# Two dense layers after an attention: a shorter activation chain, next tokens split part by part, and an even rate of weight conversion

## The chip, the cores and the metric

The kernel runs on one core of one Trainium2 chip. The metric is the time of one execution on the device in microseconds (us). The engines of the core work side by side, each through its own list of instructions in order: TensorE (PE, the matrix products), VectorE (DVE), ScalarE (ACT), GpSimd (POOL), and SyncE (SP), which here issues the transfers (DMA). Matrix products go into PSUM banks, from which VectorE and ScalarE read; all else lies in SBUF. An engine that reaches an instruction whose data or buffer is not ready waits there, and all that stands behind it in its list waits too.

## The reference, cut to what matters

```python
scores = q @ k.T / 8                       # 4 batches x 8 heads, 576 tokens, 64 wide
thresh = max(scores) - tau                 # per row
attn   = softmax(where(scores >= thresh, scores, -1e9))
x      = (attn @ v) as 2304 tokens x 512
h = x @ w_in                               # first layer, 512 -> 2048
g = where(h >= 1, h, where(h <= -1, 0, (h + 1)**2 / 4))
x = g @ w_out                              # 2048 -> 512
h = x @ w_in2                              # second layer, same sizes
out = (h * clip(h + 3, 0, 6) / 6) @ w_out2
```

## The kernel before, in words

**Numbers in two parts.** Every operand of a matrix product in the dense layers is kept as a high and a low half (`xh`/`xl` for tokens, `wih`/`wil` and `woh`/`wol` for weights, `gh`/`gl` for activations), and a product is three matrix products: high with high, high with low, low with high. So tokens and weights are *split* before use. Splitting one token part (128 rows by up to 512 tokens; a group of tokens has four parts, one for each value of `kk`) is a transfer into `xst` (three buffers), a copy on ScalarE (L521) and a subtraction on VectorE (L522).

**Weights.** Each of the 64 weight pieces (two layers, 16 slices `f`, one piece of `w_in` and one of `w_out` for each slice) is converted from 64-bit numbers. A piece takes two *halves* of work: the first (`split_a`) is two ScalarE operations (L115, L124), three VectorE ones (L125, L128, L130) and one on GpSimd (L132); the second (`split_b`) is one on ScalarE (L138) and one on GpSimd (L140). The raw pieces have three buffers, and the load of a piece is put into SyncE's list up to three pieces ahead. While the attention runs, L119 and L121 stand in place of L124 and L125.

**Order of work.** First comes the attention. From the end of its first batch on, the first layer's work for slices 0 to 9 of the first batches (groups of 256 tokens, 60 steps, `dense1`) is threaded through it. Then `dense` runs the rest of the first layer (`seq2`): 16 steps for token group 3 (512 tokens wide), 16 for group 4 (256 wide), and 6 each for groups 0, 1 and 2 (512 wide, slices 10 to 15 alone). Then it runs the second layer: 80 steps, groups in the order 3, 0, 1, 4, 2. A step takes one group and one slice: `em_h` makes twelve matrix products into one of four PSUM banks Q, then the activation (first layer: L548 VectorE, L549 ScalarE, L550 VectorE; second layer: L552 ScalarE, L553 VectorE), then the split of the result (`gh` L556 on ScalarE, `gl` L557 on GpSimd). The products with `w_out` (L581) follow two steps later (MLAG = 2) and add up in PSUM banks P; after the last slice of a group the sums are copied out (`ob`: L622, L624, L626 in the first layer, L632 and L634 in the second), and only then can the next group's products start in those banks.

**What sets the order.** The program emits a step's work in the order of the code: `ahead2` or `ahead3` (weight halves), `em_h`, the split of the next group's tokens, the products of two steps ago. A scheduler then puts each engine's list in order, by times that it models, so an engine's list is not the order of the code. In the first layer `ahead2` gives up to two halves a step, as long as the number of pieces stays under a limit: the limit rises by two pieces a step from step 20 on (in group 4, as the buffers of slices 0 to 9 come free for the second layer's weights), stops after ten steps' worth, and rises again in the last steps. In the second layer `ahead3` gives four halves a step until all are converted.

Of the kernel before, what the change touches and what calls it, by code (L numbers as in the profile page):

```python
# [10 lines left out]
ACTF = mybir.ActivationFunctionType  # L11
ALU = mybir.AluOpType
# [6 lines left out]
def kernel(  # L19
# [13 lines left out]
    V, S, G, T = nc.vector, nc.scalar, nc.gpsimd, nc.tensor  # L33
    NB, NH, SEQ, D = q.shape
    NT, DM = out.shape
    HP = NH // 2
    KD = DM // 128
    KF = DM * 4 // 128
# [9 lines left out]
    NF1 = 10  # L48
    MLAG = 2
# [16 lines left out]
    half = const.tile([128, 1], F32, name="half")  # L66
# [5 lines left out]
    def narrow(t, g):  # L72
        return t[g // 2][:, :, (g % 2) * GRP:(g % 2 + 1) * GRP]

    def f32(ap):
        return ap.bitcast(F32)

    def bank(tag):
        return ps.tile([128, 512], F32, tag=tag, name=tag)
# [104 lines left out]
    weights = Weights()  # L184
# [317 lines left out]
    xs, gs, acc, cnt = {}, {}, {}, {"h": 0, "a": 0}  # L502
    wide = {}
    H_TAGS = ["Q2"]

    def split_x(key):
        m, g, ph = key
        r = []
        for kk in range(KD):
            if ph == 1:  # L510
                if kk % 2 == 0:
                    t = mt.tile([128, 2, GRP], F32, tag="io", name="xst", bufs=2)
                    nc.sync.dma_start(out=t, in_=narrow(xd, g)[:, kk:kk + 2, :])
                pool, n, bufs, src = mt, GRP, 1, t[:, kk % 2]
            else:
                pool, n, bufs = wide["x"], WIDE[g], 2
                src = pool.tile([128, n], F32, tag="xst", name="xst", bufs=3)
                nc.sync.dma_start(out=src, in_=(x2d if m == 1 else xd)[g][:, kk, :])
            hi = pool.tile([128, n], F32R, tag=f"xh{kk}", name="xh", bufs=bufs)
            lo = pool.tile([128, n], F32R, tag=f"xl{kk}", name="xl", bufs=bufs)  # L520
            S.activation(out=hi, in_=src, func=ACTF.Copy)  # L521
            V.tensor_tensor(out=lo, in0=src, in1=f32(hi), op=ALU.subtract)  # L522
            r.append((hi, lo))
        xs[key] = r

    def pin_mlp(mm):
        if mode["att"]:
            after(mm, pe_pins[-2])

    def em_h(key, m, f):  # L530
        cnt["h"] += 1
        n = GRP if key[2] == 1 else WIDE[key[1]]
        h = bank(H_TAGS[cnt["h"] % len(H_TAGS)])[:, 0:n]
        wh, wl = wsp["i", m, f]
        x = 0
        for kk in range(KD):
            xh, xl = xs[key][kk]
            for l, r in ((wh, xh), (wh, xl), (wl, xh)):
                mm = T.matmul(h, l[:, kk * 128:(kk + 1) * 128], r, start=(x == 0), stop=(x == 3 * KD - 1))  # L539
                if x % 3 == 0:  # L540
                    pin_mlp(mm)
                x += 1
            if kk < KD - 1:
                yield 0.33
        hp_, hb = (mt, HOLD) if key[2] == 1 else (wide["g"], MLAG + 1)
        r = hp_.tile([128, n], F32, tag="r", name="r", bufs=2)
        if m == 0:
            V.tensor_scalar(out=r, in0=h, scalar1=1.0, scalar2=-1.0, op0=ALU.min, op1=ALU.max)  # L548
            S.activation(out=r, in_=r, func=ACTF.Square, scale=0.5, bias=half)  # L549
            vlast = V.tensor_tensor(out=r, in0=h, in1=r, op=ALU.max)  # L550
        else:
            S.activation(out=r, in_=h, func=ACTF.Relu, bias=three)  # L552
            vlast = V.scalar_tensor_tensor(out=r, in0=r, scalar=6.0, in1=h, op0=ALU.min, op1=ALU.mult)  # L553
        gh = hp_.tile([128, n], F32R, tag="gh", name="gh", bufs=hb)
        gl = hp_.tile([128, n], F32R, tag="gl", name="gl", bufs=hb)
        x = S.activation(out=gh, in_=r, func=ACTF.Copy)  # L556
        y = G.tensor_tensor(out=gl, in0=r, in1=f32(gh), op=ALU.subtract)  # L557
        gs[key, f] = (gh, gl)
        if not mode["att"]:
            pins.update(S=x, V=vlast, G=y)  # L560

    def blocks(m, g):

        return KD if m == 0 else WIDE[g] // 128

    def em_out(key, m, f, first, last, fin, i):

        gh, gl = gs[key, f]
        wh, wl = wsp["o", m, f]
        if first:  # L570
            if i % 2 == 0:
                acc[key, i // 2] = pair_bank(f"P{i // 2}")
        c = slice(i * 128, (i + 1) * 128)
        if m == 0:
            a = acc[key, i // 2][:, i % 2, 0:WIDE[key[1]]]
            ops = (wh[:, c], gh), (wh[:, c], gl), (wl[:, c], gh)
        else:
            a = acc[key, i // 2][:, i % 2]
            ops = (gh[:, c], wh), (gh[:, c], wl), (gl[:, c], wh)
        for x, (l, r) in enumerate(ops):  # L580
            T.matmul(a, l, r, start=(first and x == 0), stop=(last and x == 2))  # L581
        if last:
            fin(key[1], a, i)
# [30 lines left out]
    def load_part(g):  # L614
        for i in range(KD):
            pbs[g, i] = wide["p"].tile([128, WIDE[g]], F32, tag="pb", name="pb", bufs=KD)
            nc.sync.dma_start(out=pbs[g, i], in_=x2p[g][:, i, :])
# [31 lines left out]
    while o < len(outs):  # L649
        n = len(steps)  # L650
# [30 lines left out]
    def behind():  # L681

        for l in steps[n_h:]:
            for g, half, f in l:
                for _ in em_part((0, g, 1), half, f):
                    pass
                yield

    def dense(m, ph, seq, fin, ahead, following, rest=None):

        fs = {}
        for g, f in seq:
            fs.setdefault(g, []).append(f)
        splits = [(m, g, ph) for g in fs] + following

        def out_block(n, i):
            g, f = seq[n]
            em_out((m, g, ph), m, f, f == fs[g][0], f == fs[g][-1], fin, i)
            if i == blocks(m, g) - 1:
                del gs[(m, g, ph), f]  # L700

        for n, (g, f) in enumerate(seq):
            key = (m, g, ph)
            if key not in xs:
                split_x(key)
            ahead(n, g, f)
            for c in em_h(key, m, f):
                pass
            if rest is not None:
                rest(n)  # L710
            if m == 0 and g < NB - 1 and f == fs[g][-3]:
                load_part(g)
            if f == fs[g][-2]:
                for nxt in splits[splits.index(key) + 1:][:1]:
                    split_x(nxt)
            if f == fs[g][-1]:
                xs.pop(key)
            if n >= MLAG:
                for i in range(blocks(m, seq[n - MLAG][0])):
                    out_block(n - MLAG, i)  # L720
        for i in range(blocks(m, seq[-1][0])):
            for n in range(len(seq) - MLAG, len(seq)):
                out_block(n, i)
# [29 lines left out]
    fs2 = list(range(NF1, KF))  # L753
# [33 lines left out]
    NLATE = 2  # L787
# [12 lines left out]
    seq2 = [(g, f) for g in (NB - 1, NB) for f in range(KF)]  # L800
    n_free = len(seq2) - KF + MLAG + 1
    seq2 += [(g, f) for g in range(NB - 1) for f in fs2]
    n_last = len(seq2) - len(fs2) + MLAG + 1
    left = behind()
    SWITCH = MLAG + 2

    def rest(n):

        if n <= MLAG:
            for _ in range(100 if n == MLAG else 4):  # L810
                if next(left, 0) == 0:
                    break
        if n == MLAG:
            H_TAGS[:] = ["Q0", "Q1", "Q2", "Q3"]
            mt_es.close()
            wide["p"] = ctx.enter_context(tc.tile_pool(name="mt2", bufs=1, side="right"))
            wide["g2"] = ctx.enter_context(tc.tile_pool(name="g2", bufs=1, side="right"))

    def ahead2(n, g, f):
        if n == SWITCH:  # L820
            wide["g"] = wide["g2"]
        if n == SWITCH + MLAG + 1:
            g_es.close()
            late = ctx.enter_context(tc.tile_pool(name="wlate", bufs=1))
            for x in range(KF - NLATE, KF):
                wpool[x] = late
        limit = 2 * KF if n > SWITCH + MLAG else 2 * (KF - NLATE)
        limit += 2 * max(0, min(n - n_free, NF1)) + 2 * max(0, n - n_last)
        for _ in range(2):
            if weights.done < limit:  # L830
                weights.half()
        if g == NB - 1:
            weights.upto(2 * f + 2)

    def ahead3(n, g, f):
        for _ in range(4):
            weights.half()
        weights.upto(2 * KF + 2 * n + 2)

    order3 = [NB - 1, *range(NB - 2), NB, NB - 2]  # L840
# [31 lines left out]
```

## Time and profile before

| what | value |
|---|---|
| time, median of 3 runs | 1221.02 us (1218.41 to 1221.44) |
| the profiled execution: its own time | 1220.3 us |
| its span in the trace | 1218.5 us |
| TensorE busy / weight loads | 95% / 81% of the span |
| VectorE, ScalarE, GpSimd busy | 59%, 55%, 59% |
| mean granted clock of TensorE | 0.990 |

The span runs from the first to the last instruction in the trace; 1.8 us of the execution's time lie around it. Busy shares are means over stages with different limits, so they say little by themselves: the attention, up to about 515 us, has all four engines between 78% and 91% busy, and the stretch after 846 us has TensorE alone busy. TensorE's granted clock is given as a share of full speed (2.4 GHz); its only other level is half of that.

### The profile page before, as it was taken

The page shows a single profiled execution, that of the slowest core. Times are in us where ns is not written, and L with a number is a line of the kernel's source. Part 1 is how long each engine was busy: PE and PEld are TensorE (multiplying, and loading weights), DVE is VectorE, ACT ScalarE, POOL GpSimd, SP SyncE. Part 2 cuts the span into 40 slices and gives each one's busy share as a digit, 9 for nine tenths or more (in the row PEclk, how much of TensorE's full clock was granted, in tenths as well). Part 3 has the DMA queues.
Part 4 walks back from the last instruction along what each step waited for, and adds up shares of the span by engine and source line. Part 5 has one row for each costly group of instructions (what it writes and reads, how often), then busy time and mean ns, then how long its engine had stood idle before and what let it go on. Part 6 is the DMA issues. An engine that isn't in the chain of part 4 may idle for free. (4 is left out here: it accounts for less than half of the span.)

```text
span 1218.5 us, 19295 instructions
## 1 busy us (share of the span) xinstructions
PE 1160.1 (95%) x6820; PEld 992.8 (81%) x6820; DVE 715.1 (59%) x1543; ACT 667.1 (55%) x1222; POOL 724.7 (59%) x745
## 2 busy tenths in 40 slices
PE   7899999999999899989999988998999999999998
PEld 5666678998898899989889976886888888888886
DVE  6999989988888889484344797466321121121111
ACT  6777778788788688564334665345332232232222
POOL 5887699999899899665342877347522222222221
PEclk9999999999999999989999999999999999999999
DMA  6444431121121220142112454444010010010000
GB/s 161 129 129 120 135 111 51 48 77 50 49 76 46 64 72 31 53 146 74 61 53 70 120 165 133 135 135 142 1 31 26 1 43 23 1 44 1 18 1 35
DMA packets 99857, 87.08 MB, mean 71 GB/s; under 512 B 51376, under 2 KB 83632, under 8 KB 99760
## 3 DMA queue, kind: packets, MB, share of 16 engines
q1 hardware_dynamic: 99760, 85.85, 23.9%
q8 instruction: 54, 0.88, 0.3%
q14 instruction: 43, 0.35, 0.1%
HBM read 68.52 MB, written 17.30 MB: 70 GB/s over the span
## 5 line engine op out<-in xcount | busy, mean ns | idle before, releaser
L557 POOL TENSOR_TENSOR gl<-r,gh 128x512 fp32r<-128x512 f32 (+1 forms) x190 | 205.0, 1080 | 380.9 <-ACT gh L556 365.8
L539 PE MATMUL Q<-xh,wih 128*128 128x512 f32 (+1 forms) x760 | 262.3, 345 | 0.9 <-ACT xh L521 0.7
L539 PE MATMUL Q<-xl,wih 128*128 128x512 f32 (+1 forms) x760 | 259.5, 341 | 1.4 <-DVE xl L522 1.4
L539 PE MATMUL Q<-xh,wil 128*128 128x512 f32 (+1 forms) x760 | 258.8, 341 | 0.0
L553 DVE SCALAR_TENSOR_TENSOR r<-r,Q 128x512 f32<-128x512 f32 (+1 forms) x80 | 50.8, 634 | 270.4 <-ACT r L552 270.2
L539 PEld LDWEIGHTS Q<-xh,wih 128*128 128x128 f32 x760 | 145.7, 192 | 19.3 <-ACT xh L521 1.4
L539 PEld LDWEIGHTS Q<-xl,wih 128*128 128x128 f32 x760 | 145.7, 192 | 18.4 <-DVE xl L522 1.9
L334 DVE SCALAR_TENSOR_TENSOR p<-p,th,e 128x576 f32<-128x576 f32 x144 | 152.0, 1057 | 11.1 <-ACT e L330 8.9
L539 PEld LDWEIGHTS Q<-xh,wil 128*128 128x128 f32 x760 | 145.7, 192 | 15.7
L556 ACT ACTIVATE gh<-r 128x512 fp32r<-128x512 f32 (+1 forms) x190 | 99.3, 523 | 101.9 <-PE P L581 40.1
L380 POOL TENSOR_TENSOR Gl<-pf,Gh 128x512 fp32r<-128x512 f32 (+1 forms) x110 | 146.2, 1329 | 10.0 <-ACT Gh L379 3.3
L552 ACT ACTIVATE r<-Q,three 128x512 f32<-128x512 f32 (+1 forms) x80 | 51.5, 644 | 162.0 <-PE Q L539 157.8
L330 ACT ACTIVATE e<-p,nm 128x576 f32<-128x576 f32 x144 | 110.9, 772 | 34.6 <-DVE p L329 33.4
L581 PE MATMUL P<-woh,gh 128*128 128x512 f32 x288 | 112.9, 394 | 5.1 <-DVE ob L622 3.9
L329 DVE TENSOR_SCALAR_CACHE_REDUCE p<-P 128x576 f32<-128x576 f32 x144 | 107.5, 748 | 12.6 <-PE P L305 6.9
L318 PE MATMUL P<-kst,qh 128*128 128x288 f32 x320 | 99.3, 326 | 14.6 <-DVE xu L451 5.4
L581 PE MATMUL P<-wol,gh 128*128 128x512 f32 x288 | 112.8, 392 | 0.0
L581 PE MATMUL P<-woh,gl 128*128 128x512 f32 x288 | 111.3, 391 | 0.0
L132 POOL TENSOR_TENSOR w_c<-w_c,w_raw 128x512 int32<-128x512 int32 x64 | 87.8, 1371 | 35.2 <-issue 16.8
L549 ACT ACTIVATE r<-r,half 128x256 f32<-128x256 f32 (+1 forms) x110 | 62.6, 571 | 83.3 <-DVE r L548 82.8
L318 PE MATMUL P<-kst,ql 128*128 128x288 f32 x320 | 91.6, 302 | 0.3 <-DVE ql L271 0.3
L355 PE MATMUL Q<-ident,p 128*128 128x128 f32 x576 | 88.4, 276 | 1.8 <-ACT pf L376 1.3
(105 smaller groups left out, 2650.5 us busy)
## 6 DMA issues: line engine op xcount, KB each, us to landing
w_raw<-in_moe_w_in_dram SPq DMA_DIRECT2D x32, 512.0 KB, 4.1
w_raw<-in_moe_w_out_dram SPq DMA_DIRECT2D x32, 512.0 KB, 3.8
qn<-in_q_dram SPq DMA_DIRECT2D x32, 256.0 KB, 3.5
xst<-xd SPq DMA_DIRECT2D x28, 256.0 KB, 3.1
kn<-in_k_dram SPq DMA_DIRECT2D x32, 128.0 KB, 2.5
xd<-xu SPq DMA_DIRECT2D x16, 256.0 KB, 2.3
x2d<-ob SPq DMA_DIRECT2D x16, 256.0 KB, 3.7
xst<-x2d SPq DMA_DIRECT2D x16, 256.0 KB, 3.7
```

What stands on the lines that cost most here:

```text
L132: x = G.tensor_tensor(out=c.bitcast(I32), in0=c.bitcast(I32), in1=r, op=ALU.add)
L318: mm = T.matmul(s[:, e, 0:HS], l, r[:, e * HS:(e + 1) * HS], start=(x == 0), stop=(x == len(ops) - 1))
L329: V.tensor_scalar(out=p, in0=s, scalar1=-1.0, scalar2=3e38, op0=ALU.mult, op1=ALU.min, accum_out=nm)
L330: S.activation(out=e, in_=p, func=ACTF.Exp, bias=nm, scale=-1.0)
L334: V.scalar_tensor_tensor(out=p, in0=p, scalar=th, in1=e, op0=ALU.is_le, op1=ALU.mult, accum_out=zt[j][:, i:i + 1])
L355: x = T.transpose(tm[:, cc * 128:(cc + 1) * 128], p[:, cc * 128:(cc + 1) * 128], ident)
L380: G.tensor_tensor(out=lo[:, :, d], in0=f[:, 0:4, b], in1=f32(hi[:, 0:4, d]), op=ALU.subtract)
L539: mm = T.matmul(h, l[:, kk * 128:(kk + 1) * 128], r, start=(x == 0), stop=(x == 3 * KD - 1))
L549: S.activation(out=r, in_=r, func=ACTF.Square, scale=0.5, bias=half)
L556: x = S.activation(out=gh, in_=r, func=ACTF.Copy)
L557: y = G.tensor_tensor(out=gl, in0=r, in1=f32(gh), op=ALU.subtract)
L581: T.matmul(a, l, r, start=(first and x == 0), stop=(last and x == 2))
```

## The change

The first layer's activation becomes `max(min(relu(0.5 h + 0.5)^2, 1), h)`: two ScalarE operations in a row (Relu out of PSUM, then Square) and one VectorE operation (minimum, then maximum with `h` out of PSUM), in place of VectorE, ScalarE, VectorE. The next group's tokens are asked for one part in each of four steps (in a group of 16 slices at its steps 11 to 14 counted from 0, in a group of six at its steps 1 to 4), in place of all four in the step before the last. From step 20 of `seq2` on (steps counted from 0), weights are converted at one half a step in group 4, then four halves in three steps, up to slice 9 of the second layer at most, and in the second layer at two halves a step.

```diff
-    def split_x(key):
+    def split_x(key, kks=range(KD)):
         m, g, ph = key
-        r = []
-        for kk in range(KD):
+        r = xs.setdefault(key, [])
+        for kk in kks:
+            if kk < len(r):
+                continue
...
             r.append((hi, lo))
-        xs[key] = r
...
         if m == 0:
-            V.tensor_scalar(out=r, in0=h, scalar1=1.0, scalar2=-1.0, op0=ALU.min, op1=ALU.max)
-            S.activation(out=r, in_=r, func=ACTF.Square, scale=0.5, bias=half)
-            vlast = V.tensor_tensor(out=r, in0=h, in1=r, op=ALU.max)
+            S.activation(out=r, in_=h, func=ACTF.Relu, scale=0.5, bias=half)
+            S.activation(out=r, in_=r, func=ACTF.Square)
+            vlast = V.scalar_tensor_tensor(out=r, in0=r, scalar=1.0, in1=h, op0=ALU.min, op1=ALU.max)
...
-            if key not in xs:
-                split_x(key)
+            split_x(key)
...
-            if f == fs[g][-2]:
+
+            kk = fs[g].index(f) + KD + 1 - len(fs[g])
+            if 0 <= kk < KD:
                 for nxt in splits[splits.index(key) + 1:][:1]:
-                    split_x(nxt)
+                    split_x(nxt, range(kk + 1))
...
-        limit = 2 * KF if n > SWITCH + MLAG else 2 * (KF - NLATE)
-        limit += 2 * max(0, min(n - n_free, NF1)) + 2 * max(0, n - n_last)
-        for _ in range(2):
-            if weights.done < limit:
-                weights.half()
-        if g == NB - 1:
-            weights.upto(2 * f + 2)
+        if n < n_free:
+
+            limit = 2 * KF if n > SWITCH + MLAG else 2 * (KF - NLATE)
+            for _ in range(2):
+                if weights.done < limit:
+                    weights.half()
+            if g == NB - 1:
+                weights.upto(2 * f + 2)
+        else:
+
+            limit = 2 * KF + 2 * min(n - n_free, NF1)
+            for _ in range(2 if g < NB - 1 and n % 3 == 0 else 1):
+                if weights.done < limit:
+                    weights.half()
 
     def ahead3(n, g, f):
-        for _ in range(4):
-            weights.half()
+        weights.half()
+        weights.half()
         weights.upto(2 * KF + 2 * n + 2)
```

The lists of the engines show what the scheduler makes of it. In these rows a number behind Q or P tells one bank's use from the next (the numbers grow from step to step, and differ between the two kernels), and 256 is the width of group 4. First VectorE's list late in group 4, before the change:

```order
L125 TENSOR_SCALAR w_c<-w_c 128x512
L548 TENSOR_SCALAR r<-Q_9118 128x256
L128 TENSOR_SCALAR w_c<-w_c 128x512
L548 TENSOR_SCALAR r<-Q_9164 128x256
L130 SCALAR_TENSOR_TENSOR w_c<-w_raw,w_c 128x512
L550 TENSOR_TENSOR r<-Q_9118,r 128x256
L550 TENSOR_TENSOR r<-Q_9164,r 128x256
L125 TENSOR_SCALAR w_c<-w_c 128x512
L548 TENSOR_SCALAR r<-Q_9210 128x256
L128 TENSOR_SCALAR w_c<-w_c 128x512
L130 SCALAR_TENSOR_TENSOR w_c<-w_raw,w_c 128x512
```

And the same place after it (L551 is the new VectorE operation of the activation):

```order
L125 TENSOR_SCALAR w_c<-w_c 128x512
L128 TENSOR_SCALAR w_c<-w_c 128x512
L130 SCALAR_TENSOR_TENSOR w_c<-w_raw,w_c 128x512
L551 SCALAR_TENSOR_TENSOR r<-r,Q_9088 128x256
L551 SCALAR_TENSOR_TENSOR r<-r,Q_9125 128x256
L125 TENSOR_SCALAR w_c<-w_c 128x512
L128 TENSOR_SCALAR w_c<-w_c 128x512
L130 SCALAR_TENSOR_TENSOR w_c<-w_raw,w_c 128x512
L551 SCALAR_TENSOR_TENSOR r<-r,Q_9167 128x256
L551 SCALAR_TENSOR_TENSOR r<-r,Q_9204 128x256
```

Where a step had a whole first half of a conversion and two operations of its own, two steps now share one conversion and have one operation each.

Next VectorE's list at the end of group 4, where the tokens of the next group (group 0) are split (L522, after the change L524). Before:

```order
L130 SCALAR_TENSOR_TENSOR w_c<-w_raw,w_c 128x512
L550 TENSOR_TENSOR r<-Q_9407,r 128x256
L548 TENSOR_SCALAR r<-Q_9464 128x256
L522 TENSOR_TENSOR xl<-xst,xh 128x512 x2
L125 TENSOR_SCALAR w_c<-w_c 128x512
L128 TENSOR_SCALAR w_c<-w_c 128x512
L550 TENSOR_TENSOR r<-Q_9464,r 128x256
L130 SCALAR_TENSOR_TENSOR w_c<-w_raw,w_c 128x512
L522 TENSOR_TENSOR xl<-xst,xh 128x512
```

After:

```order
L130 SCALAR_TENSOR_TENSOR w_c<-w_raw,w_c 128x512
L551 SCALAR_TENSOR_TENSOR r<-r,Q_9343 128x256
L524 TENSOR_TENSOR xl<-xst,xh 128x512 x3
L551 SCALAR_TENSOR_TENSOR r<-r,Q_9386 128x256
L125 TENSOR_SCALAR w_c<-w_c 128x512
L128 TENSOR_SCALAR w_c<-w_c 128x512
L524 TENSOR_TENSOR xl<-xst,xh 128x512
```

The code asks for the four parts in four steps, but in the list three of them still stand together, in the step before the last, and the fourth comes in the last.

Last, ScalarE's list in the attention, where the first layer's steps are threaded in (L330 is the exponential, L376 and L379 take transposed tiles out of PSUM and split them). Before:

```order
L379 ACTIVATE Gh<-pf_102 128x5x128
L330 ACTIVATE e<-p,nm 128x576
L549 ACTIVATE r<-r,half 128x256
L376 ACTIVATE pf_103<-Q_6080 128x512
L330 ACTIVATE e<-p,nm 128x576
L420 ACTIVATE fold<-Q_6043 64x256
L379 ACTIVATE Gh<-pf_103 128x5x128
L556 ACTIVATE gh<-r 128x256
```

After (L549 is now the Relu, L550 the Square, L557 the copy that was L556):

```order
L376 ACTIVATE pf_102<-Q_6028 128x512
L549 ACTIVATE r<-Q_6024,half 128x256
L379 ACTIVATE Gh<-pf_102 128x5x128
L550 ACTIVATE r<-r 128x256
L330 ACTIVATE e<-p,nm 128x576
L557 ACTIVATE gh<-r 128x256
L376 ACTIVATE pf_103<-Q_6080 128x512
```

A step of the first layer now stands three times in ScalarE's list where it stood twice, and its three entries stand closer together.

## Rows read from the trace of the kernel before

**Rows 1.** First line of the page.

```profile
span 1218.5 us, 19295 instructions
```

**Rows 2.** Busy us by stretch: PE, PEld, DVE, ACT, POOL; clock, DMA share, GB/s.

```profile
155.00:515.00 360.00, 340.98 (x2681) 322.74 (x2682) 305.96 (x842) 282.82 (x516) 327.10 (x377) 1.00 0.21 59
...
540.00:650.00 110.00, 110.00 (x596) 95.79 (x595) 49.17 (x75) 46.49 (x79) 49.95 (x42) 1.00 0.22 69
650.00:690.00 40.00, 40.00 (x313) 38.86 (x312) 23.21 (x44) 21.34 (x43) 23.43 (x23) 1.00 0.32 98
690.00:760.00 70.00, 60.36 (x286) 49.00 (x285) 60.06 (x79) 43.21 (x77) 54.23 (x41) 0.96 0.47 143
760.00:818.00 58.00, 58.00 (x255) 47.97 (x254) 31.38 (x45) 25.35 (x42) 23.03 (x18) 0.99 0.46 138
818.00:846.00 28.00, 23.46 (x95) 18.35 (x94) 17.62 (x26) 13.70 (x24) 19.34 (x16) 0.94 0.49 151
```

**Rows 3.** Chain that ended last, in time: start us, us, what.

```profile
1120.69 1.43 PE Q L539 x12
...
1147.99 2.72 PE Q L539 x12
```

**Rows 4.** Waits from 690 to 760 us: us in total, times, longest.

```profile
PE P L581 <- ACT gh L556: 4.2, 3, 2.2
...
PE P L581 <- DVE ob L626: 2.4, 1, 2.4
PE P L581 <- DVE ob L622: 2.3, 1, 2.3
```

**Rows 5.** Waits from 818 to 846 us.

```profile
PE P L581 <- DVE ob L622: 3.9, 2, 3.7
```

**Rows 6.** The conversion's operations: count, busy us, mean ns, idle before them.

```profile
L132 POOL TENSOR_TENSOR w_c<-w_c,w_raw 128x512 int32<-128x512 int32 x64 | 87.8, 1371 | 35.2 <-issue 16.8 <-DVE w_c L130 14.1 <-ACT Gf L372 1.4
...
L130 DVE SCALAR_TENSOR_TENSOR w_c<-w_raw,w_c 128x512 uint32<-128x512 uint32 x64 | 64.3, 1004 | 1.2
...
L128 DVE TENSOR_SCALAR w_c<-w_c 128x512 uint32<-128x512 uint32 x64 | 48.2, 753 | 1.1
...
L140 POOL TENSOR_TENSOR wil<-w_c,wih 128x512 fp32r<-128x512 f32 x32 | 45.2, 1415 | 4.8 <-ACT wih L138 4.7
...
L115 ACT ACTIVATE w_raw<-w_raw 128x512 int32<-128x512 uint32 x64 | 43.0, 673 | 19.1 <-DMA w_raw<-in_moe_w_out_dram 11.5 <-DMA w_raw<-in_moe_w_in_dram 7.3
...
L125 DVE TENSOR_SCALAR w_c<-w_c 128x512 f32<-128x512 f32 x44 | 33.5, 762 | 19.7 <-ACT w_c L124 19.6
...
L124 ACT ACTIVATE w_c<-w_raw 128x512 f32<-128x512 f32 x44 | 29.4, 669 | 13.9 <-POOL wol L140 8.5 <-POOL wil L140 5.3
...
L138 ACT ACTIVATE wih<-w_c 128x512 fp32r<-128x512 f32 x32 | 20.0, 626 | 19.4 <-POOL w_c L132 19.0
```

**Rows 7.** The activation and its split, by shape, as in rows 6.

```profile
L557 POOL TENSOR_TENSOR gl<-r,gh 128x512 fp32r<-128x512 f32 x98 | 129.0, 1318 | 309.8 <-ACT gh L556 302.2 <-issue 7.4
...
L557 POOL TENSOR_TENSOR gl<-r,gh 128x256 fp32r<-128x256 f32 x92 | 76.0, 827 | 71.1 <-ACT gh L556 63.6 <-DVE w_c L128 2.6 <-DVE w_c L130 1.2
...
L549 ACT ACTIVATE r<-r,half 128x256 f32<-128x256 f32 x76 | 38.1, 503 | 30.9 <-DVE r L548 30.5
...
L556 ACT ACTIVATE gh<-r 128x256 fp32r<-128x256 f32 x92 | 37.7, 411 | 21.5 <-DVE r L550 10.7 <-DVE r L553 5.4 <-PE P L581 5.2
...
L548 DVE TENSOR_SCALAR r<-Q 128x256 f32<-128x256 f32 x76 | 31.4, 414 | 16.0 <-PE Q L539 9.0 <-POOL gl L557 6.4 <-issue 0.4
...
L552 ACT ACTIVATE r<-Q,three 128x256 f32<-128x256 f32 x16 | 7.6, 475 | 20.7 <-PE Q L539 20.2 <-POOL gl L557 0.5
...
L553 DVE SCALAR_TENSOR_TENSOR r<-r,Q 128x256 f32<-128x256 f32 x16 | 6.7, 421 | 38.2 <-ACT r L552 38.2
```

**Rows 8.** Waits of ScalarE from 150 to 515 us.

```profile
ACT r L549 <- DVE r L548: 13.5, 15, 2.1
```

**Rows 9.** Idle time of ScalarE before L521, by what ended it: us, times.

```profile
  DMA xst<-x2d: 14.8, 5
```

More of the change, by code (lines that the diff above doesn't have):

```diff
@@ L802 @@
     seq2 += [(g, f) for g in range(NB - 1) for f in fs2]
-    n_last = len(seq2) - len(fs2) + MLAG + 1
     left = behind()
```

## The prediction

> **What bounds the kernel now.** I read the views in this order: the table of stretches, the waits of TensorE in the stretches where it idles, then the groups of instructions by shape, to see what the other engines ask of a step.
>
> The table of stretches [rows 2] is to be read by TensorE's busy time against the length. From 540 to 690 us and from 760 to 818 us TensorE is busy all the time: nothing that the other engines save there is worth anything. Between them stands a stretch of 70 us in which it is busy for 60.36 and its mean granted clock is 0.96, and from 818 to 846 us it is busy for 23.46 of 28 at a clock of 0.94. In the attention, from 155 to 515 us, it is busy for 340.98 of 360, with VectorE at 306 (85%), ScalarE at 283 (79%) and GpSimd at 327 (91%).
>
> The waits say who was late. From 690 to 760 us the products with `w_out` wait for `gh` of ScalarE (4.2 us) and for copies out of the banks P, `ob`, of VectorE (2.4 and 2.3 us) [rows 4]; from 818 to 846 us for `ob` (3.9 us) [rows 5]. These are no slow operations: both engines work through their lists in order and reach `gh` and `ob` late. Why they are late is found in the load of a step. Twelve products 256 wide take 1.43 us, 512 wide 2.72 us [rows 3], and a step has twelve for `em_h` and twelve for `w_out`: 2.86 us in group 4, 5.44 us elsewhere. Two halves of a conversion a step cost VectorE 762 + 753 + 1004 = 2519 ns, GpSimd 1371 + 1415 = 2786 ns and ScalarE 673 + 669 + 626 = 1968 ns [rows 6]. With the step's own activation at 256 [rows 7] that makes for VectorE 2519 + 2 x 414 = 3.35 us (the closing maximum taken like L548), for GpSimd 2786 + 827 = 3.61 us, for ScalarE 1968 + 503 + 411 = 2.88 us. All three are over 2.86 us. From step 20 to step 31 GpSimd falls behind by 12 x 0.75 = 9 us, VectorE by 12 x 0.49 = 6 us, and the wide steps that follow, still with two halves each, pay that back slowly: hence 690 to 760 us. At the start of the second layer four halves a step ask GpSimd for 2 x 2786 + 1318 = 6.9 us in a step of 5.44 us [rows 3, 6, 7], and VectorE has the last copies out of the first layer in the same list: hence 818 to 846 us.
>
> **The change part by part.**
>
> *The even rate.* What stands to be won is TensorE's idle time in the two stretches, (70 - 60.36) + (28 - 23.46) = 14.2 us, and what its clock lost there, (1 - 0.96) x 70 + (1 - 0.94) x 28 = 4.5 us; in both stretches the clock is below full only where the engine has also idled, and it is 0.99 or 1.00 in the unbroken ones [rows 2]. Together 18.7 us. After the change a step of group 4 has one half: VectorE 1260 + 421 = 1.68 us, GpSimd 1393 + 827 = 2.22 us, ScalarE 984 + 475 + at most 503 + 411 = 2.37 us, all under 2.86 us. The wide steps of the first layer have 4/3 halves: GpSimd 1857 + 1318 = 3.2 us of 5.44. The second layer starts with two halves: GpSimd 2786 + 1318 = 4.1 us of 5.44. The steps from 540 to 650 us have this same load of two halves on wide steps, and there TensorE never idled [rows 2]; that is my row for what is left over. It holds neither the copies `ob` nor a split of tokens, so I leave 2 us of the 18.7 in place: four group ends remain (0, 1, 2 and 4 of the first layer), at which VectorE has up to four copies to make before TensorE can go on, and the largest waits for one were 2.4 and 3.7 us [rows 4, 5]. Bounds: 0 us gained if the lateness only moves to other steps, 18.7 if all goes. Value taken: 16.7 us.
>
> What is moved: 64 pieces remain 64, and so do their loads. The halves that went into steps 20 to 39 now reach to the end of the first layer, 36 halves (18 pieces) from step 20 to step 49, and 28 are left for the second layer: at two a step done in its step 13. Slice f is needed in step f; at step n, 18 + n + 1 second-layer pieces stand ready against 2n + 2 needed, so the forced catching-up (`upto`) never acts. A load is issued three pieces ahead, 16 us in the second layer, so transfers are not what is late. On SyncE's list the loads pass the token parts, which wait for VectorE to free a buffer; the parts' own places hardly move.
>
> *The parts of the next tokens.* In the lists three of the four parts still stand together, so this edit changes little. The cover that makes it cheap either way is the lag of two steps between `em_h` and the products with `w_out`. ScalarE's waits for the part that is loaded last, 14.8 us over five groups [rows 9], lie mostly in stretches where TensorE is never idle [rows 2]. I take 0; bounds: 3 us lost if a part's transfer holds up `gh` once at each of two group ends, 3 us gained if the spreading acts.
>
> *The activation.* From 540 us on it lies under a busy TensorE, beside what is counted above. In the attention 60 steps pass through it. VectorE loses 60 x 414 ns and pays 7 ns more for the other operation: -24.4 us, from 306 to 282 of 360. ScalarE loses 503 and gains a Relu out of PSUM, 475 as the second layer's has it, and a Square without a bias operand, which no row shows: between the copy's 411 and the 503 of the Square with one [rows 7]. That is 383 to 475 ns a step, 23 to 28.5 us, from 283 to about 308 of 360 (86%). I take the copy's 411. GpSimd, the fullest engine, keeps its 91%. A chain of four engines' turns becomes one of three, and the 13.5 us in which ScalarE stood before L549 waiting for VectorE [rows 8] have no successor of that kind, for the Relu reads PSUM and TensorE's result; instead ScalarE can wait for TensorE there, with exponentials queued behind it. TensorE idles 19 us in this stretch, the most that a better flow can give [rows 2]; the worst is that ScalarE's 23 to 28.5 us all come onto the path. Between these ends the nearest row is the balance of the two engines, which only changes sides (85 and 79% become 78 and 86%). I take a gain of 1 us for the shorter chain.
>
> ScalarE's row for Relu at 256 is 475 ns against 414 on VectorE [rows 7]. The Trainium skill, page "ScalarE: Activation LUTs", section "Rules for kernel authors", says to put relu, max and min on VectorE and not on ScalarE; these rows agree in direction, and by that rule alone the attention would lose, as in the third rival below.
>
> Sum: the profiled execution took 1220.3 us, 1.8 more than its span [rows 1]. 1220.3 - 16.7 - 0 - 1 = 1202.6 us; the median of the runs shown is 0.7 above the profiled one, so 1203 us.
>
> **The rivals.**
>
> *Part of it stays.* The parts stand together, `ob` still queues behind a conversion's three operations, and half of the 18.7 us remains. For it: at a group's end the list still has such rows. Against it: all engines are below the step's time. It gives 1220.3 - 9.4 = 1211 us.
>
> *The attention gains too.* With VectorE at 78% the tiles that TensorE waits for come sooner; half of its 19 idle us go: 1203 - 9 = 1194 us. Against it: GpSimd stays at 91%.
>
> *ScalarE becomes the bound of the attention.* Its place is the stretch from 155 to 515 us, its price the 23 to 28.5 us of added work. It decides when the exponentials wait behind Relu and Square, that is when ScalarE's busy share passes GpSimd's 91% or its waits for TensorE exceed the 13.5 us that it is rid of. It gives 1220.3 - 16.7 + 26 = 1230 us, slower than before. Against it: 86% is still under GpSimd's 91%.
>
> *The change doesn't do what it says.* The scheduler evens nothing out, and the lateness turns up in steps that were free before (760 to 818 us): 1220 us. Against it: VectorE's list in group 4 shows one conversion for two steps.
>
> **How the numbers follow.** Forecast 0.55 (1197 to 1208), part of it stays 0.19, the attention gains too 0.10, no effect 0.07, ScalarE as the bound 0.09. What a measurement of this kernel can tell from no change is about 0.3%, 3.7 us: faster is below 1217.4. The first three cases are faster: 0.84; no effect is the same: 0.07; slower 0.09. The range from 1192 to 1216 takes in the forecast, the partial case and most of the attention's gain, and leaves out the last two.
>
> **What would show it.** Right: in the stretches of the changed kernel that answer to 690 to 760 and 818 to 846 us TensorE idles 2 us or less and the clock is 1.00; no wait for `ob` above 1 us; three `xl` still stand in a row. In the attention VectorE's busy time falls by 24 us, ScalarE's rises by 23 to 28, and TensorE's idle time stays near 19 us. Wrong: waits for `ob` or `gh` at other group ends of the first layer or in the first 14 steps of the second; idle time of TensorE in the attention that differs by more than 5 us; a time outside 1192 to 1216 us.

## The result, and the profile after

The changed kernel takes 1206.38 us (median of 4 runs, 1205.04 to 1207.25) against 1219.72 us of the kernel before on the same chip (4 runs): a ratio of 0.9895, interval 0.9865 to 0.9926. That is faster, 3 us above the forecast of 1203 us and inside the range. The profiled execution took 1205.04 us.

The first lines of the page of the changed kernel, to be read against [rows 1] and the table of busy shares:

```profile
span 1203.3 us, 19343 instructions
...
PE 1151.6 (96%) x6820; PEld 990.1 (82%) x6820; DVE 672.0 (56%) x1433; ACT 707.8 (59%) x1332; POOL 717.2 (60%) x745
```

The table of stretches of the changed kernel, columns as in [rows 2]:

```profile
155.00:515.00 360.00, 335.61 (x2629) 317.99 (x2630) 293.65 (x791) 292.67 (x556) 321.50 (x374) 1.00 0.21 57
...
540.00:650.00 110.00, 108.41 (x604) 95.03 (x603) 39.80 (x55) 57.13 (x102) 52.35 (x44) 1.00 0.23 72
650.00:690.00 40.00, 40.00 (x293) 38.09 (x292) 18.12 (x29) 24.09 (x52) 18.34 (x19) 1.00 0.29 93
690.00:760.00 70.00, 70.00 (x376) 60.77 (x376) 42.30 (x64) 48.84 (x89) 42.12 (x34) 1.00 0.45 143
760.00:818.00 58.00, 58.00 (x258) 48.04 (x257) 33.88 (x47) 32.30 (x54) 32.93 (x25) 1.00 0.46 148
818.00:846.00 28.00, 28.00 (x125) 23.21 (x124) 14.88 (x18) 16.12 (x28) 20.58 (x16) 1.00 0.31 94
```

From 650 to 846 us TensorE is now busy in every microsecond at a granted clock of 1.00, where in two of these stretches it was busy for 60.36 of 70 and 23.46 of 28 us. The waits of [rows 4, 5] have no successors: the list of TensorE's waits from 690 to 850 us is empty. But the attention moved the other way: TensorE is busy there for 335.61 us instead of 340.98, with less work on VectorE and GpSimd and more on ScalarE. (That is 93% of the stretch, and was 95%: the 78% to 91% of the section on the time before hold for the other three engines, not for TensorE.)

The two stretches are cut at fixed times, and the programs drift against them, so I also cut each trace at its own events, by the start times of the matrix products: A, from the first product of the first layer's first step (at 141 to 145 us, in the attention) to the first product of token group 3 after it; B, from there to the first product of step 16 of the second layer; C, the rest to the last product. C, to the start of that product, is 312.2 to 312.3 us in every kernel of this study. These are worked out from single profiles; A varies by 2.0 us among the four kernels whose code up to the end of A differs in nothing that matters (before, rate_alone, parts_alone, old_act), by 2.1 us between the changed kernel and act_alone, and by 3.0 us between before_3550 and rate_3550, which run the same attention. So a difference in A of less than 3 us tells nothing by itself. Nearly all of this noise arises before the start of the 61st exponential (L330; 205 us in the kernel before); the last column is what is left of A from there on, and in it kernels of the same attention agree within 0.3 to 0.7 us.

| kernel (what of the change it has) | share | A, us | B, us | median, us | A from the 61st exponential, us |
|---|---|---|---|---|---|
| before | 0.3484 | 413.8 | 343.7 | 1219.7 to 1221.1 | 352.5 |
| changed (all) | 0.3484 | 421.4 | 321.5 | 1206.4 | 360.9 |
| rate_alone (even rate) | 0.3484 | 412.8 | 321.5 | 1198.1 | 352.2 |
| parts_alone (parts) | 0.3484 | 413.2 | 343.3 | 1220.5 | 352.4 |
| act_alone (activation) | 0.3484 | 423.5 | 343.2 | 1229.9 | 361.6 |
| old_act (rate, parts) | 0.3484 | 414.8 | 321.5 | 1198.3 | 352.4 |
| att_old (all, old activation in the attention) | 0.3484 | 416.7 | 321.5 | 1199.3 | 354.6 |
| square_dve (all, Square on VectorE there) | 0.3484 | 429.2 | 321.5 | 1214.2 | 368.7 |
| gh_dve (all, `gh` on VectorE there) | 0.3484 | 424.9 | 321.5 | 1206.8 | 360.3 |
| before_3400 | 0.34 | 421.6 | 341.6 | 1223.5, one run | 357.4 |
| after_3400 | 0.34 | 424.3 | 321.5 | 1206.7, one run | 361.4 |
| before_3550 | 0.355 | 411.3 | 345.0 | 1217.1, one run | 350.6 |
| after_3550 | 0.355 | 412.3 | 321.5 | 1197.6, one run | 349.1 |
| rate_3550 (even rate) | 0.355 | 414.3 | 321.8 | 1196.4 | 351.1 |

So the result is -22.2 us in B and +7.6 us in A: 1220.3 - 22.2 + 7.6 = 1205.7, against 1205.0 measured in the profiled execution.

### The profile page after: what moved, and what is told of

It is laid out like the page before. It is cut to its first block, busy times and chain, and to the rows that moved or that the text cites. A ratio compares the mean times of both kernels' runs of the same rounds, so it can differ in the third digit from the quotient of the medians.

```text
span 1203.3 us, 19343 instructions
## 1 busy us (share of the span) xinstructions
PE 1151.6 (96%) x6820; PEld 990.1 (82%) x6820; DVE 672.0 (56%) x1433; ACT 707.8 (59%) x1332; POOL 717.2 (60%) x745
## 4 chain that ended last, share of the span: by engine, by line
PE 70%; POOL 12%; DVE 8%; issue 4%; ACT 3%; DMA 2%; SPq 0%; POOLq 0%; DVEq 0%; ACTq 0%
PE Q L540 29%; PE P L582 26%; POOL Gl L380 6%; PE Q L597 4%; PE P L318 3%; PE Q L408 3%; POOL Gh L381 2%; DVE p L334 2%; PE Q L355 2%; PE Q L410 2%; DVE p L329 2%; POOL vst L294 1%; POOL gl L558 1%; POOL ksp L234 1%; DVE xl L524 1%
## 5 line engine op out<-in xcount | busy, mean ns | idle before, releaser
L558 POOL TENSOR_TENSOR gl<-r,gh 128x512 fp32r<-128x512 f32 (+1 forms) x190 | 202.5, 1066 | 374.9 <-ACT gh L557 355.1
L557 ACT ACTIVATE gh<-r 128x512 fp32r<-128x512 f32 (+1 forms) x190 | 99.6, 524 | 120.1 <-PE P L582 50.5
L334 DVE SCALAR_TENSOR_TENSOR p<-p,th,e 128x576 f32<-128x576 f32 x144 | 149.0, 1036 | 12.7 <-ACT e L330 10.3
L330 ACT ACTIVATE e<-p,nm 128x576 f32<-128x576 f32 x144 | 110.9, 772 | 33.3 <-DVE p L329 31.8
L551 DVE SCALAR_TENSOR_TENSOR r<-r,Q 128x256 f32<-128x256 f32 (+1 forms) x110 | 54.5, 496 | 121.1 <-ACT r L550 119.8
```

Of the source, the lines that this page charges most:

```text
L330: S.activation(out=e, in_=p, func=ACTF.Exp, bias=nm, scale=-1.0)
L334: V.scalar_tensor_tensor(out=p, in0=p, scalar=th, in1=e, op0=ALU.is_le, op1=ALU.mult, accum_out=zt[j][:, i:i + 1])
L551: vlast = V.scalar_tensor_tensor(out=r, in0=r, scalar=1.0, in1=h, op0=ALU.min, op1=ALU.max)
```

## The experiments

**One part of the change at a time.** Four kernels, on one chip with 19 runs of the kernel before (1220.97 us). rate_alone is the kernel before with the last hunk of the diff alone (`ahead2`, `ahead3`):

```diff
+            limit = 2 * KF + 2 * min(n - n_free, NF1)
+            for _ in range(2 if g < NB - 1 and n % 3 == 0 else 1):
...
-        for _ in range(4):
-            weights.half()
+        weights.half()
+        weights.half()
```

> The even rate alone, on the kernel before. If the two stretches of idle TensorE came from the rate alone: all of them go, TensorE idles under 1 us between 560 us and the end of the first 16 steps of the second layer, the attention stays as before (last product of scores at 493 us), and the time is 1219.7 - 19 to 22 = 1198 to 1201 us. If the activation's lighter VectorE share was needed as well: waits for ob of 2 us or more remain at group ends, and the time is 1205 us or more.

Measured: 1198.09 us, ratio 0.9807 (0.9786 to 0.9828): the whole gain and more. Its two stretches:

```profile
690.00:760.00 70.00, 70.00 (x336) 59.02 (x335) 52.70 (x76) 39.32 (x68) 40.58 (x31) 1.00 0.48 151
...
818.00:846.00 28.00, 28.00 (x126) 23.17 (x125) 23.59 (x22) 15.40 (x26) 23.03 (x17) 1.00 0.36 110
```

TensorE waits for nothing in either, although the old activation keeps VectorE busier from 690 to 760 us (52.70) than it is in the changed kernel (42.30). The even rate needs no help from the other two parts.

parts_alone is the kernel before with the hunks of `split_x` and `dense`:

```diff
-            if f == fs[g][-2]:
+            kk = fs[g].index(f) + KD + 1 - len(fs[g])
+            if 0 <= kk < KD:
```

> The next tokens' parts alone, on the kernel before. If the scheduler makes nothing of it, as the lists say: 1219.7 us within 3 us, with both idle stretches as before. If the burst of four parts had a share in the stalls: the idle time at 700 to 705 us and 745 to 757 us shrinks and the time falls by 3 us or more.

Measured: 1220.45 us, ratio 0.9991 (0.9976 to 1.0006): no change. TensorE idles in both stretches much as in [rows 2]:

```profile
690.00:760.00 70.00, 61.20 (x280) 49.17 (x279) 60.79 (x79) 42.90 (x75) 53.94 (x40) 0.95 0.50 150
...
818.00:846.00 28.00, 23.78 (x95) 18.85 (x94) 18.34 (x25) 15.13 (x25) 20.61 (x16) 0.88 0.49 148
```

act_alone is the kernel before with the three lines of the activation:

```diff
-            V.tensor_scalar(out=r, in0=h, scalar1=1.0, scalar2=-1.0, op0=ALU.min, op1=ALU.max)
-            S.activation(out=r, in_=r, func=ACTF.Square, scale=0.5, bias=half)
-            vlast = V.tensor_tensor(out=r, in0=h, in1=r, op=ALU.max)
+            S.activation(out=r, in_=h, func=ACTF.Relu, scale=0.5, bias=half)
+            S.activation(out=r, in_=r, func=ACTF.Square)
+            vlast = V.scalar_tensor_tensor(out=r, in0=r, scalar=1.0, in1=h, op0=ALU.min, op1=ALU.max)
```

> The activation alone, on the kernel before. If the changed kernel's 7 us of delay at the start of the wide steps come from the activation: the first wide step starts at 565 us as there, against 558 before. In group 4 GpSimd's load stays at 3.6 us for a step of 2.86, so most of the idle TensorE from 690 to 760 and 818 to 846 us remains (10 us or more of the 14): 1219.7 + 7 - 4 = 1223 us. If the lighter VectorE alone cures the stalls: under 5 us of idle time there, and about 1208 us.

Measured: 1229.87 us (8 runs, 1225.13 to 1236.03), ratio 1.0070 (1.0046 to 1.0094): slower, by 8.9 us, and by 7 more than the first case of the expectation. Its stretches:

```profile
155.00:515.00 360.00, 335.76 (x2614) 316.53 (x2613) 292.14 (x790) 292.88 (x556) 321.40 (x374) 0.99 0.21 57
...
690.00:760.00 70.00, 62.66 (x331) 52.27 (x331) 55.16 (x63) 47.85 (x92) 52.53 (x41) 0.95 0.43 137
760.00:818.00 58.00, 54.37 (x227) 43.92 (x226) 29.82 (x41) 28.49 (x48) 22.43 (x17) 0.94 0.48 142
818.00:846.00 28.00, 28.00 (x125) 23.21 (x124) 16.38 (x23) 16.90 (x30) 21.26 (x17) 1.00 0.48 147
```

The attention is that of the changed kernel. After it the stalls of the old rate are still there, the second only moved from its stretch into the one before (54.37 of 58): B is 343.2 us against 343.7, so the 4 us that I had expected from the lighter VectorE did not come. VectorE's lower load there is worth nothing while GpSimd still has more than a step's work in a step.

old_act is the changed kernel with those three lines put back (the minus lines above in place of the plus lines).

> Even rate and parts with the old activation. If the new activation costs the attention and the start of the wide steps 7 us and buys nothing later: 1206.4 - 7 = 1199 us, faster than the changed kernel, with the first wide step at 558 us. If the new activation is needed to keep VectorE from falling behind: idle TensorE of 3 us or more comes back after 690 us, and the time is 1203 us or more.

Measured: 1198.27 us, ratio 0.9812 (0.9794 to 0.9829), as rate_alone. So at the given order the new activation costs the changed kernel 8.1 us (1206.38 - 1198.27; by the ratios to the kernel before, which ran beside each, 10 us), and A says where: 421.4 against 414.8 us.

**Where the activation costs, and whether it is ScalarE's load.** Three kernels, on one chip with 11 runs of the kernel before (1221.07 us). att_old has the old activation while the attention runs, the new one after it:

```diff
+            if mode["att"]:
+                V.tensor_scalar(out=r, in0=h, scalar1=1.0, scalar2=-1.0, op0=ALU.min, op1=ALU.max)
...
+            else:
+                S.activation(out=r, in_=h, func=ACTF.Relu, scale=0.5, bias=half)
```

> The changed kernel with the old activation while the attention runs and the new one after it. If the new activation's cost lies in the attention alone: the last score product is at 490 to 493 us as with the old activation, and the time is that of the even rate alone, 1198 to 1200 us. If it also costs at the start of the wide steps, after the attention: 1 to 3 us more, 1200 to 1202 us. If it was needed after the attention to relieve VectorE: below 1197 us.

Measured: 1199.27 us, ratio 0.9831 (0.9812 to 0.9850). Most of the cost lies in the attention; after it, where 64 of the first layer's steps still pass through the new activation, it costs nothing that a median shows.

square_dve gives ScalarE's added work back: in the attention the square is `r * r` on VectorE.

```diff
-            S.activation(out=r, in_=r, func=ACTF.Square)
+            if mode["att"]:
+                V.tensor_tensor(out=r, in0=r, in1=r, op=ALU.mult)
+            else:
+                S.activation(out=r, in_=r, func=ACTF.Square)
```

> The changed kernel with the Square on VectorE (r times r) while the attention runs, so that ScalarE and VectorE have as many operations for a step as before, in the new formula. If ScalarE's added load was the cost, by Gh that comes late and GpSimd that stands before Gl: GpSimd's waits for Gh fall from 9.4 us back to 3 to 5, and the time to 1198 to 1201 us. If the place of the steps in the list is the cost, or the Relu that ScalarE reads out of PSUM: attention as slow as in the changed kernel, 1205 to 1208 us.

Measured: 1214.17 us, ratio 0.9957 (0.9941 to 0.9972): slower than the changed kernel. The square on VectorE, from the groups of instructions by shape in the attention (columns as in [rows 6]), and the stretch of the attention:

```profile
L551 DVE TENSOR_TENSOR r<-r 128x256 f32<-128x256 f32 x43 | 27.4, 637 | 3.3 <-ACT r L549 1.5 <-POOL Gl L380 1.5
```

```profile
155.00:515.00 360.00, 328.23 (x2539) 309.22 (x2539) 316.55 (x829) 274.14 (x497) 322.19 (x363) 0.99 0.21 56
```

ScalarE is down to 274.14 us, below the 282.82 of [rows 2], and TensorE has still lost: VectorE went to 316.55, for its square takes 637 ns where ScalarE's takes 413.

gh_dve leaves the activation as changed, and has VectorE copy `gh` in the attention in ScalarE's place, so that both engines come near their old loads:

```diff
-        x = S.activation(out=gh, in_=r, func=ACTF.Copy)
+        if mode["att"]:
+            x = V.tensor_scalar(out=gh, in0=r, scalar1=1.0, scalar2=0.0, op0=ALU.mult, op1=ALU.add)
+        else:
+            x = S.activation(out=gh, in_=r, func=ACTF.Copy)
```

> The changed kernel with the copy gh on VectorE while the attention runs: ScalarE has Relu and Square for a step, VectorE the minimum-maximum and gh, two each as before. If ScalarE's added load was the cost: as with the Square moved, 1198 to 1201 us. If only the Square's place between Relu and the rest counts: no better than the changed kernel, 1205 to 1208 us.

Measured: 1206.82 us, ratio 0.9885 (0.9865 to 0.9905): the same as the changed kernel, with ScalarE at 278 us in the attention. That ScalarE's added work makes it late, so far my explanation, is not borne out: relieved of it in two ways, the attention stays as long or gets longer, and GpSimd's waits for `Gh`, 9.4 us in the changed kernel, are 11.2 and 10.7 us where 3 to 5 were expected. It is not refuted either: both variants put work on VectorE (316.55 and 315.44 us, above the 305.96 of [rows 2]), and both change the order of the lists as well. A clean relief, work that is simply gone, was not tried.

**The same operations in another order.** `share` (L767, after the change L769) is the credit that each step of the attention gives to the first layer's work; it is 0.3484 in both kernels. Another value threads the same steps through the attention at other places. Four kernels with one run each, the kernel before beside them 1219.98 us, one run too:

```diff
-    share = 0.3484
+    share = 0.3400
```

and 0.3550 in the other two. The expectations set two theories against each other: T1, that the load of the new operations costs, and T2, that their place in the lists does.

> The kernel before with the share of TensorE's time that the attention leaves to the first layer set from 0.3484 to 0.34, which shifts where every step is threaded in. If the attention's length hangs on the accident of the order: the start of the first wide step moves by 3 us or more either way against 558 us. If it is set by the engines' load: 555 to 561 us.

> The kernel before with the share set to 0.355. As with 0.34: by the order's accident a shift of 3 us or more either way in the start of the first wide step, by the load 555 to 561 us.

> The changed kernel with the share set to 0.34. If ScalarE's added load costs the attention its 6 to 8 us: the first wide step starts 5 to 10 us later than in the kernel before with the same share. If the cost was an accident of one order: within 3 us of it, or earlier.

> The changed kernel with the share set to 0.355. As with 0.34: by ScalarE's load the first wide step starts 5 to 10 us later than in the kernel before with the same share; by an accident of one order within 3 us of it, or earlier.

Measured: 1223.50, 1217.12, 1206.72 and 1197.57 us. By the measure that was put down for it, the start of the first wide step, the kernel before moves by +5.5 and -4.3 us against its 557.8, more than the 3 us put down as the mark of the order; but the changed kernel starts its wide steps 3.3 and 4.0 us after the kernel before with the same share, between the two cases put down (within 3, or 5 to 10). Of the 4.0, 3.0 stand before the first step of the first layer, where no new operation has run. In A, the new activation costs 424.3 - 421.6 = 2.6 us at 0.34, 6.6 to 7.6 at 0.3484 (421.4 against 414.8 of old_act and 413.8 of before) and 412.3 - 411.3 = 1.0 us at 0.355. The last column, which leaves most of the noise out, parts them more clearly: 4.0 us at 0.34, 8.4 to 9.4 at 0.3484, and -1.5 at 0.355. The changed kernel's attention with its TensorE waits at a share of 0.355, its stretch first:

```profile
155.00:515.00 360.00, 339.94 (x2635) 320.52 (x2635) 293.28 (x795) 295.19 (x562) 321.34 (x375) 0.99 0.21 59
```

```profile
PE Q L410 <- POOL Gl L380: 9.0, 12, 1.6
PE Q L410 <- DVE xu L422: 2.3, 2, 2.1
```

ScalarE does as much as in the changed kernel (295.19 against 292.67), and TensorE is busy 4.3 us longer.

**The even rate at that share.** The kernel before with the last hunk and `share = 0.3550`, to weigh after_3550 by its old activation (five runs):

```diff
-    share = 0.3484
+    share = 0.3550
```

> The kernel before with the even rate alone (old activation, old parts) and a share of 0.355 for the threading of the first layer's steps in place of 0.3484. T1, the new activation costs 5 to 10 us in the attention whatever the order: this kernel is 5 to 10 us faster than the changed kernel at the same share (1197.6 us in one look), so 1188 to 1193 us. T2, the cost hangs on where the steps are threaded and is near nothing at this share: within 3 us of 1197.6, most likely 1195 us, which is the even rate alone at 0.3484 (1198.1) less the 2.9 us by which the kernel before was faster at 0.355 (1217.1 against 1220.0). By both, TensorE waits for nothing from 690 to 850 us, and its wide steps after the attention begin about 411 us after the first step's first product.

Measured: 1196.35 us, ratio 0.9816 (0.9796 to 0.9835); A is 414.3 us, 3.3 more than the expectation's 411. It stands 1.2 us from after_3550's single run, and not 5 to 10 us below it, and by the ratios to the kernel before, which ran beside each, the two are the same (1197.57 / 1219.98 = 0.9816); from the 61st exponential on the new activation is 2.0 us the faster (349.1 against 351.1). That speaks for T2, on one run of the changed kernel at this share. It is no faster than rate_alone (0.9807) either, so a share that suits one activation is not a gain by itself. rate_alone, old_act and rate_3550 all beat both kernels; the cheapest good version is the even rate alone.

## Why the prediction came out as it did

**The even rate: the mechanism as predicted, the term too small.** Predicted -16.7 of 18.7 us; B shows -22.2 in the changed kernel, rate_alone and old_act alike. Nothing stayed: from 560 us on the list of TensorE's waits in the changed kernel is empty, so no wait for `ob` or `gh` follows, and my 2 us for what is left were not needed. The other 3.5 us are time that idle time and clock don't add up to. Taken from the starts of the products, each against its usual spacing, the kernel before lost 14.5 us from 690 to 760 us and 6.9 from 818 to 846, 21.4 together: around a stall the products also start further apart while the engine counts as busy. Why they do, the trace doesn't tell. That GpSimd and VectorE had more than a step's work in a step is borne out by the cure: the same operations, spread evenly, stall nothing. "Part of it stays" is out.

**The parts: right.** 0 predicted, 0.9991 measured. The waits of ScalarE for the transfer of the last part fell in the changed kernel, and no engine that mattered noticed. The line answers to [rows 9], here for the whole time from 150 us on, where the kernel before has the same 14.8:

```profile
ACT xh L523 <- DMA xst<-x2d: 6.2, 3, 3.1
```

**The activation in the attention: the step that failed.** Predicted a gain of 1 us; it cost 6.6 to 7.6 in A. Two terms of it were wrong. The count: 60 steps pass through the stretch, I wrote, but only 45 have run by 515 us (46 in the kernel before). The sizes of the operations were right; the changed kernel's rows for the attention:

```profile
L549 ACT ACTIVATE r<-Q,half 128x256 f32<-128x256 f32 x45 | 21.1, 469 | 3.5 <-PE Q L540 3.1
L550 ACT ACTIVATE r<-r 128x256 f32<-128x256 f32 x45 | 18.6, 413 | 0.3
L557 ACT ACTIVATE gh<-r 128x256 fp32r<-128x256 f32 x45 | 18.5, 411 | 6.2 <-DVE r L551 6.1
L551 DVE SCALAR_TENSOR_TENSOR r<-r,Q 128x256 f32<-128x256 f32 x45 | 18.3, 408 | 3.8 <-ACT r L550 2.7 <-POOL gl L558 0.8
```

The Square without a bias operand takes 413 ns, the copy's 411 as I took it, and the Relu 469 for 475. ScalarE's cost is 469 + 413 - 503 = 379 ns a step, 17 us for 45 steps; the stretch shows +9.9 on ScalarE and -12.3 on VectorE, less than the -24 and +23 of the prediction, also because the changed kernel is 5 us behind at 515 us.

The second wrong term is the balance itself. I weighed busy shares (85 and 79% to 78 and 86%) and found them to change sides, so little should happen. ScalarE's waits before L549 did what was said: 13.5 us for VectorE [rows 8] became 3.1 for TensorE, in the first of the rows above. But TensorE's idle time rose from 19.0 to 24.4 us, over the 5 us that I had named as the sign of a wrong step. The waits of TensorE from 150 to 515 us, before and then after (the two that grew most):

```profile
PE Q L410 <- POOL Gl L380: 3.2, 5, 1.2
...
PE Q L410 <- DVE xu L422: 1.3, 2, 0.9
```

```profile
PE Q L410 <- POOL Gl L380: 9.5, 11, 1.3
PE Q L410 <- DVE xu L422: 4.4, 4, 1.7
```

And the largest wait of GpSimd in the same stretch, the changed kernel alone (before, it stood at 3.3 us):

```profile
POOL Gl L380 <- ACT Gh L379: 9.4, 10, 1.7
```

The chain reads: ScalarE's `Gh` later, GpSimd's `Gl` later, TensorE waits. That looks like the third rival, ScalarE as the bound, at a quarter of its price; but its own marks are missing. ScalarE is at 292.67 of 360 us (81%), not above 91%, and its waits for TensorE before L549, the place that the prediction named, are 3.1 us, not 13.5. (Before all its operations they went from 12.5 to 17.4 us, so it does wait for TensorE more, by 4.9 us.) And at 0.355 the same long wait for `Gl` (9.0 us) goes with a fast attention: the wait that grew is not the measure of the loss.

What the runs do show is a place. By the order of the exponentials (L330) the changed kernel keeps up with the one before, at times 4 us ahead, until 353 us, falls 6.7 us behind by 377 us, and ends the attention 5 us behind. That stretch before, after, and in after_3550:

```profile
350.00:380.00 30.00, 28.65 (x235) 27.81 (x234) 25.90 (x71) 24.29 (x43) 28.41 (x35) 1.00 0.28 75
```

```profile
350.00:380.00 30.00, 26.81 (x211) 25.20 (x210) 22.95 (x64) 22.58 (x42) 24.87 (x28) 1.00 0.19 57
```

```profile
350.00:380.00 30.00, 27.75 (x225) 26.86 (x224) 24.80 (x66) 24.88 (x47) 27.31 (x33) 1.00 0.28 78
```

In the second line all four engines do less than in the first, GpSimd 3.5 us less: none is the bound, each waits in turn for the next. Nor is this stretch a mark of the new activation as such: the exponentials of after_3550 are 5.5 us behind those of before_3550 at the 61st, 11.6 at the worst, and 6.4 at the last. The rest, some 2 us, falls behind the attention's end, where TensorE enters group 3. From 500 to 560 us the largest waits on two tiles, in the kernel before, in the changed kernel, and in after_3550 (there on the second alone):

```profile
PE Q L539 <- DVE xl L522: 1.4, 2, 1.1
...
PE Q L539 <- DVE r L550: 0.2, 1, 0.2
```

```profile
PE Q L540 <- DVE xl L524: 3.0, 1, 3.0
PE Q L540 <- DVE r L551: 2.0, 2, 1.6
```

```profile
PE Q L540 <- DVE r L551: 0.8, 1, 0.8
```

att_old still has these two waits (2.9 and 2.2 us), and from the 61st exponential on it takes 354.6 us against old_act's 352.4. So the same operations cost 8.4 us or more, 4.0 us or nothing, by how their rows fall among the attention's rows; a fixed price for their load, as in T1, is not what the three shares show, with one run each at two of them. What the prediction's sum lacked is a term for this order: it put it at nothing, without a reason. Which instruction's place starts the loss at 353 us stays open: no run moved one instruction alone.

**The rule that spoke against the change.** By the Trainium skill, page "ScalarE: Activation LUTs", section "Rules for kernel authors", which says to put relu on VectorE and gives its reason for bf16, the activation should have lost. At 0.3484 it did, by 8 us; at 0.355 it did not, in one run, with ScalarE as busy. The rows, in float32, agree with the rule for one operation (469 against 414 ns), and do not bear out that this decides the kernel's time.

**After the attention: right.** From 540 us on the activation lies under a busy TensorE; B is 321.5 us with either activation.

**The sum.** -16.7 and -1 were predicted, -22.2 and +7.6 came. Two errors of 5.5 and 8.6 us against each other left 3 us. That the time was nearly met, with one step of the wrong sign, is luck.

## What to carry to other kernels

Where a steady stream of side work stalls the main engine, compare each engine's work per step with the step's time, stretch by stretch: that found the overload, and evening it out won all of it back. Where four engines are all between 79 and 95% busy and wait for each other in turn, an exchange of work between two of them can't be priced from busy shares; time it at two or three orders of the same work (here a change of `share` by 2 to 3%) more than once each, before the operation is given credit or blame. And split a change into its parts even when the whole has won: here the even rate alone is 8 us faster than the three parts together.

## What the runs showed of the hardware

A stall can cost more than the idle time that it leaves: the two here cost 21.4 us by the spacing of the products, 18.7 by idle time and clock, and without them B is 22.2 us shorter. The product of a tile with itself on VectorE (128x256, both operands in SBUF) took 637 ns in square_dve, where the operation with one operand in PSUM took 408 and ScalarE's Square 413 in the changed kernel; why it takes longer was not isolated. And the same code repeats closely even where the engines wait for each other: the exponentials of rate_alone start 2.9 us before those of the kernel before, to 0.1 us, from 165 us to the last, and C repeats to 0.1 us in fourteen traces. What varies from trace to trace lies mostly ahead of that: the stretch ahead of the first step, in which no kernel here has a changed operation, differs by 3.8 us.
